# A decode step of two attention and two MLP layers on one core: each layer gets its own list of loads of keys and values, with second copies of some blocks in DRAM

## The chip, the cores and the metric

The kernel runs on one core of one Trainium2 chip. The time is the device time of one execution in microseconds (us). Before the change it is 1343.44 us, the median of 3 runs (1343.42 to 1343.6). In the profile TensorE is PE, its weight loads PEld, VectorE DVE, ScalarE ACT, GpSimd POOL, and the engine that issues most DMAs SP. All rows of the profile come from one profiled execution.

## What is computed

One token of width 640 passes through attention, an MLP, the same attention again and the same MLP again. Both attention layers read the same cache of keys and the same cache of values: 32 heads, 8192 positions, 128 wide, in float32, 134 MB each.

```python
H, Sk, Dh = 32, 8192, 128           # x is (1, 1, 640)
def _A_ref(x, k_cache, v_cache, wq, wo):
    q = heads_of(x @ wq)
    scores = jnp.einsum("bhqd,bhkd->bhqk", q, k_cache) * (Dh ** -0.5)
    p = _softmax(scores, axis=-1)
    o = jnp.einsum("bhqk,bhkd->bhqd", p, v_cache)
    return joined(o) @ wo
def _B_ref(x, w1, w2):
    return jnp.maximum(x @ w1, 0) @ w2

x = x + _A_ref(_layernorm(x), k_cache, v_cache, wq, wo)
x = x + _B_ref(_layernorm(x), w1, w2)
x = x + _A_ref(_layernorm(x), k_cache, v_cache, wq, wo)
x = x + _B_ref(_layernorm(x), w1, w2)
```

## The kernel before

**What is loaded.** The cache doesn't fit into SBUF, so all of it is read from DRAM in the first layer and, but for a part that stays, once more in the second. A head has 8.4 MB: four pieces of keys and four of values, each 128 partitions by 2048 elements (1024 KB). A load ("unit") is one DMA that moves several pieces, with one contiguous row for each partition: 6 pieces are a load of 128x12288 elements (6144 KB), 4 are 128x8192 (4096 KB), 2 are 128x4096 (2048 KB). The host lays the cache out in DRAM in the order of the units, so that each unit is one block there. `UNITS` lists the units of each head, the same for both layers: by pieces or parts of them for heads 0, 1, 28, 29, 30 and 31, whole keys and whole values for heads 2, 3 and 24 to 27, and for heads 4 to 23 units that run over the ends of heads (`PAIR`, `TRIPLE`).

**The order of heads** is `HEADS`: 0 to 31 in the first layer; 31 down to 24, 12 to 23, 4 to 11, 3, 2, 1, 0 in the second. Heads 30 and 31 and three small units of head 29 (`KEPT`) stay in SBUF from the first layer to the second. Most of the first piece of head 24's keys is parked in PSUM by ACT (`PARKED`, lines 526 and 195) and copied back in the second layer, so that its load there is 128x6272 instead of 128x8192.

**The ring.** Units go to a ring of 4248 places of 8 elements a partition. `place` finds room: units of 12288 elements in three slots of 1536 places (the third reaches into the place of `w2`, which is free in the middle of a layer), smaller ones wherever they fit. `pump` issues the next loads on SP's queue, in the order of `todo`, as far as `place` finds room; `release` is called behind the last instruction that reads a piece, frees its place and calls `pump`. So a load is issued when PE has read what lay in its place; nothing else holds it, but for the eight DMA semaphores, which are used in turn.

**The work of a head.** `scores` (line 516) multiplies the pieces of the keys by the query on PE; the maximum, the exponentials and the transposes run on DVE and ACT (lines 531, 545, 552); `values` (line 570) multiplies the pieces of the values; `output` (lines 587 to 614) joins them. Between these stand small steps of the next queries (440, 454), of the output projection (621, 482) and of the MLP's weights (672). The MLP closes each layer. The weights of queries and projections are loaded by ACT's queue into `both_t`, one group of four heads ahead. The MLP's `w2` is loaded into the ring at each layer's end, and while the first layer's MLP runs, four units of head 29 for the second layer are loaded beside the ring (line 231).

Of the kernel before, what the change touches and what calls it, by code (L numbers as in the profile page):

```python
# [15 lines left out]
P = 128  # L16
D = 640
H = 32
SK = 8192
# [21 lines left out]
UNITS = {h: WHOLE for h in range(H)}  # L41
UNITS[0] = HALVES[:2] + LAST
UNITS[1] = HALVES
UNITS[29] = [
# [10 lines left out]
]  # L55
UNITS[30] = HALVES
UNITS[28] = [("k", K_ALL[:1]), ("k", K_ALL[1:2])] + HALVES[1:]
UNITS[31] = HALVES[:2] + LAST
# [5 lines left out]
TRIPLE = [  # L64
    [(0, "k", K_ALL), (0, "v", V_ALL[:2])],
    [(0, "v", V_ALL[2:]), (1, "k", K_ALL)],
    [(1, "v", V_ALL), (2, "k", K_ALL[:2])],
    [(2, "k", K_ALL[2:]), (2, "v", V_ALL)],
]
UNITS = {  # L70
    h: [[(h, kind, piece) for piece in pieces] for kind, pieces in units]
    for h, units in UNITS.items()
}
OWNER = {h: h for h in range(H)}
for first, together in [(4, TRIPLE), (7, TRIPLE), (10, PAIR)] + [(h, TRIPLE) for h in (12, 15, 18, 21)]:
    for h in range(first, first + len(together) - 1):
        UNITS[h], OWNER[h] = [], first
    UNITS[first] = [
        [(first + i, kind, piece) for i, kind, pieces in unit for piece in pieces]
        for unit in together  # L80
    ]
ORDER = [(h, i) for h in range(H) for i in range(len(UNITS[h]))]
HEADS = [list(range(H)), [*range(31, 23, -1), *range(12, 24), *range(4, 12), 3, 2, 1, 0]]
GROUPS = [[heads[a] // HG for a in range(0, H, HG)] for heads in HEADS]
KEPT = [(29, 0), (29, 1), (29, 6)]
BY_WO = KEPT[0]
# [7 lines left out]
PARKED = (24, 0)  # L94
# [8 lines left out]
def size(u):  # L103
    return sum(wide(kind, piece) for _, kind, piece in UNITS[u[0]][u[1]])
# [22 lines left out]
def decode_kernel(ctx: ExitStack, tc: tile.TileContext, x, kv, wq, wo, wqo, w1, w2, out):  # L127
# [15 lines left out]
    kept = [u for u in ORDER if u[0] > KEPT[0][0] or u in KEPT]  # L143
# [16 lines left out]
    def place(layer, u, n):  # L160
# [8 lines left out]
        if layer == 0 and u in kept and (u in KEPT or u[0] == 30 and UNITS[30][u[1]][0][1] == "k"):  # L169
            low, high = (EDGE, RING) if u in KEPT else (FLAT, EDGE)  # L170
# [8 lines left out]
    def pump():  # L179
        while todo:  # L180
# [7 lines left out]
            stays = PARK_ROW if (layer, u) == (1, PARKED) else 0  # L188
# [69 lines left out]
    def pieces_of(L, h, kind):  # L258
# [3 lines left out]
        if L:  # L262
            units.sort(key=lambda i: (h, i) not in kept)
# [876 lines left out]
```

## Time and profile before

| | |
|---|---|
| time, median of 3 runs | 1343.44 us |
| profiled execution, span | 1340.6 us |
| outside the span (the difference) | 2.8 us |
| mean granted clock of TensorE | 0.820 |
| busy: PE, PEld, DVE, ACT | 874.0, 255.5, 290.2, 62.6 us |
| DMA traffic | 571.70 MB in 24546 packets |

The first layer's attention and MLP end at about 704 us of the span, the second's at its end. The span is that of the profiled execution alone, and the times of the runs are measured around it. Of the view by lines, the two groups that fill PE are the keys and the values:

```profile
L516 PE MATMUL ps<-ring,spread_q 128*32 128x512 f32 (+3 forms) x2088 | 332.7, 727 | 149.2 <-DMA ring<-in_kv 148.6
L570 PE MATMUL outs<-ring,p 128*4 128x512 f32 (+3 forms) x2080 | 310.6, 732 | 164.1 <-DMA ring<-in_kv 95.7
```

The columns are line, engine, operation, what is written and read, the count; behind the bar the busy time and the mean in ns; then the idle time of the engine before them, and what ended most of it.

### The profile page before, as it was taken

What the parts mean: (1) busy time and instruction counts of PE and PEld (TensorE: products, weight loads), DVE (VectorE), ACT (ScalarE), POOL (GpSimd) and SP (SyncE); (2) the same over time, 40 slices, a digit from 0 to 9 for tenths busy, and PEclk for the clock granted to TensorE, in tenths of its full rate; (3) what the DMA queues carried; (4) which work ended last, traced back from release to release, by engine and by line L of the source; (5) the groups of instructions that cost most, each with busy time, mean ns of one, the idle gap of its engine ahead of it and who ended that gap; (6) DMA issues with size and microseconds to landing.
All of it is one profiled execution on the core that took longest, in us unless ns stands there. A gap on an engine that the chain in (4) does not pass through costs nothing.

```text
span 1340.6 us, 13403 instructions
## 1 busy us (share of the span) xinstructions
PE 874.0 (65%) x5806; PEld 255.5 (19%) x5806; DVE 290.2 (22%) x956; ACT 62.6 (5%) x155; POOL 2.9 (0%) x10
## 2 busy tenths in 40 slices
PE   5463575767657656676688755657566666567687
PEld 2110121111111111112243211112111111111123
DVE  2120121211212112223123212221221212212222
ACT  0000000000000000000000000000000000000000
POOL 0000000000000000000000000000000000000000
PEclk8686787988777887788799977887778787888789
DMA  9999999999999999999999999999999999999998
GB/s 395 431 435 430 442 423 437 429 428 437 432 434 429 428 439 426 433 425 415 425 396 425 430 435 433 432 433 431 433 429 434 432 428 433 437 427 436 425 424 333
DMA packets 24546, 571.70 MB, mean 426 GB/s; under 512 B 2724, under 2 KB 2984, under 8 KB 6952
## 3 DMA queue, kind: packets, MB, share of 16 engines
q1 hardware_dynamic: 21464, 529.31, 92.1%
q10 hardware_dynamic: 3024, 41.53, 7.3%
q8 instruction: 46, 0.75, 0.2%
q14 instruction: 12, 0.10, 0.0%
HBM read 570.83 MB, written 0.00 MB: 426 GB/s over the span
## 4 chain that ended last, share of the span: by engine, by line
DMA 67%; PE 27%; DVE 4%; ACT 1%; issue 1%; SPq 0%; ACTq 0%; DVEq 0%
DMA ring<-in_kv 66%; PE ps L516 10%; PE outs L570 9%; PE side L672 1%; DMA ring<-in_w 1%; DVE p L591 1%; PE acc L621 1%; PE side L440 1%; ACT p L545 1%; DVE h_t L531 1%; PE small L536 1%; PE small L604 1%; PE side L454 1%; DVE p L552 0%; DVE h_t L537 0%
## 5 line engine op out<-in xcount | busy, mean ns | idle before, releaser
L516 PE MATMUL ps<-ring,spread_q 128*32 128x512 f32 (+3 forms) x2088 | 332.7, 727 | 149.2 <-DMA ring<-in_kv 148.6
L570 PE MATMUL outs<-ring,p 128*4 128x512 f32 (+3 forms) x2080 | 310.6, 732 | 164.1 <-DMA ring<-in_kv 95.7
L531 DVE TENSOR_REDUCE h_t<-ps 128x1 f32<-128x512 f32 x64 | 44.3, 691 | 365.4 <-PE ps L516 365.4
L570 PEld LDWEIGHTS outs<-ring,p 128*4 128x4 f32 x2080 | 50.6, 95 | 348.4 <-issue 233.8
L516 PEld LDWEIGHTS ps<-ring,spread_q 128*32 128x32 f32 x2088 | 63.9, 124 | 277.5 <-issue 188.8
L545 ACT ACTIVATE p<-ps,h_t 128x512 f32<-128x512 f32 x63 | 43.3, 687 | 1161.2 <-DVE h_t L537 1161.2
L552 DVE STREAM_TRANSPOSE p<-p 128x128 f32<-128x128 f32 x256 | 79.8, 312 | 63.9 <-ACT p L545 57.2
L587 DVE TENSOR_SCALAR p<-outs,ind 128x128 f32<-128x128 f32 x64 | 22.5, 351 | 317.2 <-PE outs L570 317.2
L604 PE MATMUL small<-ones,p 128*128 128x1 f32 (+1 forms) x128 | 25.3, 267 | 97.4 <-DVE p L591 97.4
L591 DVE SCALAR_TENSOR_TENSOR p<-outs,ind,p 128x128 f32<-128x128 f32 x188 | 66.0, 351 | 6.7
L536 PE MATMUL small<-ident,h_t 128*128 128x128 f32 x128 | 32.7, 339 | 40.1 <-DVE h_t L531 39.9
L604 PEld LDWEIGHTS small<-ones,p 128*128 128x128 f32 x128 | 19.9, 195 | 159.7 <-DVE p L591 158.9
L672 PE MATMUL side<-w_t,wct 128*128 128x448 f32 (+1 forms) x80 | 45.3, 651 | 0.0
L452 DVE TENSOR_SCALAR q_row<-side,ln_r 128x128 f32<-128x128 f32 x56 | 19.5, 349 | 106.0 <-PE ps L516 59.0
L440 PE MATMUL side<-both_t,ln_xc 128*32 128x512 f32 x140 | 37.3, 844 | 0.0
L536 PEld LDWEIGHTS small<-ident,h_t 128*128 128x128 f32 x128 | 20.0, 196 | 89.0 <-DVE h_t L531 85.5
L621 PE MATMUL acc<-both_t,o_cols 128*64 128x320 f32 x220 | 34.6, 458 | 0.0
L454 PEld LDWEIGHTS side<-sel,q_row 128*128 128x128 f32 x112 | 19.3, 216 | 56.3 <-DVE q_row L452 29.9
L537 DVE TENSOR_REDUCE h_t<-small 128x1 f32<-128x128 f32 x64 | 18.7, 292 | 35.4 <-PE small L536 35.4
L454 PE MATMUL side<-sel,q_row 128*128 128x1 f32 x112 | 24.1, 284 | 0.3 <-DVE q_row L452 0.2
L621 PEld LDWEIGHTS acc<-both_t,o_cols 128*64 128x64 f32 x220 | 15.5, 147 | 29.4 <-issue 17.7
L672 PEld LDWEIGHTS side<-w_t,wct 128*128 128x128 f32 x80 | 13.5, 211 | 32.4 <-issue 32.4
(148 smaller groups left out, 219.5 us busy)
## 6 DMA issues: line engine op xcount, KB each, us to landing
ring<-in_kv SPq DMA_DIRECT2D x50, 6144.0 KB, 35.0
ring<-in_kv SPq DMA_DIRECT2D x23, 4096.0 KB, 33.2
ring<-in_kv SPq DMA_DIRECT2D x29, 2048.0 KB, 27.7
both_t<-in_wqo ACTq DMA_DIRECT2D x12, 2560.0 KB, 24.7
ring<-in_kv SPq DMA_DIRECT2D x4, 5120.0 KB, 34.6
ring<-in_kv SPq DMA_DIRECT2D x9, 1024.0 KB, 23.9
w_t<-in_w ACTq DMA_DIRECT2D x1, 4320.0 KB
ring<-in_kv SPq DMA_DIRECT2D x5, 768.0 KB, 29.5
```

The lines of the kernel that those rows point to most:

```text
L440: nc.tensor.matmul(pq[32 * strip : 32 * strip + 32], xc[:, c : c + 1].to_broadcast([P, 32]), wq_t[:, c], start=c < 4, stop=c in (1, 2, 3, ...
L454: nc.tensor.matmul(mine[:, :1], row, one_of_each, start=True, stop=True, skip_group_check=True)
L516: nc.tensor.matmul(hd.ps[32 * g : 32 * g + 32, c : c + n], spread_q[:, 3 - r : 35 - r], tile_of[:, at + g * n : at + (g + 1) * n], start=f ...
L531: nc.vector.tensor_reduce(hd.nm, hd.ps, AX.X, ALU.max, negate=True)
L536: nc.tensor.matmul(pt[:, :P], hd.nm.to_broadcast([P, P]), ident, start=True, stop=True)
L545: nc.scalar.activation(hd.p, hd.ps, AF.Exp, bias=hd.low, scale=scale, accum_out=hd.l)
L552: nc.vector.transpose(hd.all_p[:, b * P : (b + 1) * P], hd.p[:, b * P : (b + 1) * P])
L570: nc.tensor.matmul((hd.out if r0 < 2 else hd.out_2)[32 * g : 32 * g + 4, r0:r1].rearrange("p r d -> p (r d)"), hd.all_p[:, 32 * i : 32 * i ...
L591: nc.vector.scalar_tensor_tensor(oc, hd.out[:, r], ind[:, r : r + 1], oc, op0=ALU.mult, op1=ALU.add)
L604: nc.tensor.matmul(pt[:, :n], part, mask.to_broadcast([P, n]), start=i == 0, stop=i == len(parts) - 1,)
L621: nc.tensor.matmul(acc[64 * g : 64 * g + 64, : 2 * DR], col.to_broadcast([P, 64]), wt[:, 2 * DR * g : 2 * DR * (g + 1)], start=first, stop ...
L672: nc.tensor.matmul(pt[:, :n], wct[:, c], w1_t[:, c, f : f + n], start=(c == 0), stop=(c == NB - 1),)
```

## The change

The list of units is no longer one for both layers. `FIRST` and `SECOND` are the loads of the two layers, each a list of units, and `UNIT` holds what each unit consists of. A new function `cut` lays the pieces of several heads in a line and cuts it into units of six pieces (6144 KB), also across the ends of heads.

- First layer: heads 0 to 3 are one line, cut into a first unit of two pieces and five of six (before: single loads of 256 to 4096 KB). Heads 24 to 26 are four units of six (before: six units of 4096 KB). Heads 27 to 31 are as before.
- Second layer: heads 29 and 28 are as before. Heads 27, 26 and 25 are four units of six, in the order in which this layer takes them; head 24 is as before. Heads 3 and 2 are units of 6, 6 and 4 pieces, the keys of head 1 are one unit of 4096 KB, and its values and head 0 are as before.
- Heads 10 and 11 are units of 6, 6 and 4 pieces in both layers (before: 5, 5 and 6).

A block that is cut differently in the two layers lies in DRAM twice: this holds for heads 0 to 3 and 24 to 27, 67 MB more in DRAM. The bytes that are loaded are the same, and so is the order of heads. The loads of keys and values on SP are 116 instead of 130: 63 instead of 73 in the first layer, 53 instead of 57 in the second.

```diff
-UNITS = {h: WHOLE for h in range(H)}
-UNITS[0] = HALVES[:2] + LAST
-UNITS[1] = HALVES
+SIX = 6
+UNIT = {}
+def pieces_in_line(heads):
+    return [(h, kind, piece) for h in heads for kind, all_of in (("k", K_ALL), ("v", V_ALL)) for piece in all_of]
+def units_of(h, units):
+    n = sum(u[0] == h for u in UNIT)
+    for i, unit in enumerate(units):
+        UNIT[h, n + i] = unit
+    return [(h, n + i) for i in range(len(units))]
+def alone(h, units):
+    return units_of(h, [[(h, kind, piece) for piece in pieces] for kind, pieces in units])
+def cut(heads, first=0):
+    line = pieces_in_line(heads)
+    ends = [0] * bool(first) + [*range(first, len(line), SIX), len(line)]
+    return units_of(heads[0], [line[a:b] for a, b in zip(ends, ends[1:])])
...
-PAIR = [
-    [(0, "k", K_ALL), (0, "v", V_ALL[:1])],
-    [(0, "v", V_ALL[1:]), (1, "k", K_ALL[:2])],
-    [(1, "k", K_ALL[2:]), (1, "v", V_ALL)],
-]
...
+MIDDLE = [cut(heads) for heads in ([4, 5, 6], [7, 8, 9], [10, 11], [12, 13, 14], [15, 16, 17], [18, 19, 20], [21, 22, 23])]
...
+FIRST = cut([0, 1, 2, 3], 2) + sum(MIDDLE, []) + cut([24, 25, 26]) + alone(27, WHOLE) + sum(ENDS.values(), [])
+KEPT = [(29, 0), (29, 1), (29, 6)]
+SECOND = [u for u in ENDS[29] if u not in KEPT] + ENDS[28] + cut([27, 26, 25])
+PARKED += alone(24, WHOLE)[:1]
+SECOND += [PARKED[1], (24, PARKED[1][1] + 1)]
+SECOND += sum(MIDDLE[3:] + MIDDLE[:3], []) + cut([3, 2])
+SECOND += alone(1, [("k", K_ALL)] + HALVES[2:]) + alone(0, HALVES[:2] + LAST)
+ORDER = list(UNIT)
...
-    todo = [(0, u) for u in ORDER if u != BY_WO]
+    todo = [(0, u) for u in FIRST if u != BY_WO]
     n_first = len(todo)
-    todo += [(1, (h, i)) for h in HEADS[1] for i in range(len(UNITS[h])) if (h, i) not in kept]
+    todo += [(1, u) for u in SECOND]
...
-    kv = np.empty(H * P * SK * 2, k.dtype)
+    kv = np.empty(8 * P * sum(size(u) for u in ORDER), k.dtype)
```

Three places of SP's queue show what moves. At the program's start, before (`in_wq` and `in_wo` are the first query and projection weights, `in_kv` the cache):

```order
L274 DMA both_t<-in_wq 128x2560
L189 DMA ring<-in_kv 128x4096 x3
L189 DMA ring<-in_kv 128x2048
L189 DMA ring<-in_kv 128x1536
L189 DMA ring<-in_kv 128x512
L189 DMA ring<-in_kv 128x4096 x4
L286 DMA both_t<-in_wo 128x2560
L189 DMA ring<-in_kv 128x8192 x4
```

and with the change:

```order
L282 DMA both_t<-in_wq 128x2560
L201 DMA ring<-in_kv 128x4096
L201 DMA ring<-in_kv 128x12288 x2
L294 DMA both_t<-in_wo 128x2560
L201 DMA ring<-in_kv 128x12288 x13
```

Heads 0 to 3 take 14 loads before and 6 with the change, of which the first is the same. The second half of head 0's keys now comes in one load with all of its values.

At the start of the second layer, before (the first rows are the end of head 29 and head 28, then heads 27 to 24, and from 12288 on head 12 and the next):

```order
L189 DMA ring<-in_kv 128x1536
L189 DMA ring<-in_kv 128x2048
L189 DMA ring<-in_kv 128x4096
L189 DMA ring<-in_kv 128x2048 x2
L189 DMA ring<-in_kv 128x4096 x3
L189 DMA ring<-in_kv 128x8192 x6
L189 DMA ring<-in_kv 128x6272
L189 DMA ring<-in_kv 128x8192
L189 DMA ring<-in_kv 128x12288 x24
```

and with the change:

```order
L201 DMA ring<-in_kv 128x1536
L201 DMA ring<-in_kv 128x2048
L201 DMA ring<-in_kv 128x4096
L201 DMA ring<-in_kv 128x2048 x2
L201 DMA ring<-in_kv 128x4096 x3
L201 DMA ring<-in_kv 128x12288 x4
L201 DMA ring<-in_kv 128x6272
L201 DMA ring<-in_kv 128x8192
L201 DMA ring<-in_kv 128x12288 x26
```

Six loads of heads 27 to 25 became four. The first of the six was placed over values of head 30; the first of the four takes that place and the next 512 places, where the last values of head 29 lie.

At the second layer's end, before (heads 10 and 11 from the rows of 10240 on, then 3, 2, 1 and 0):

```order
L189 DMA ring<-in_kv 128x12288 x24
L189 DMA ring<-in_kv 128x10240 x2
L189 DMA ring<-in_kv 128x12288
L189 DMA ring<-in_kv 128x8192 x4
L189 DMA ring<-in_kv 128x4096 x7
L189 DMA ring<-in_kv 128x2048
L189 DMA ring<-in_kv 128x1536
L189 DMA ring<-in_kv 128x512
L222 DMA ring<-in_w 128x1920
```

and with the change:

```order
L201 DMA ring<-in_kv 128x12288 x26
L201 DMA ring<-in_kv 128x8192
L201 DMA ring<-in_kv 128x12288 x2
L201 DMA ring<-in_kv 128x8192 x2
L201 DMA ring<-in_kv 128x4096 x5
L201 DMA ring<-in_kv 128x2048
L201 DMA ring<-in_kv 128x1536
L201 DMA ring<-in_kv 128x512
L234 DMA ring<-in_w 128x1920
```

Of head 1's keys, which came in two halves of 128x4096, one load of 128x8192 is left. On PE four matmuls of head 0's last values are gone, since that piece is no longer cut; DVE, ACT and POOL have the same instructions in the same order.

More of the change, by code (lines that the diff above doesn't have):

```diff
@@ L55 @@
 ]
-UNITS[30] = HALVES
-UNITS[28] = [("k", K_ALL[:1]), ("k", K_ALL[1:2])] + HALVES[1:]
-UNITS[31] = HALVES[:2] + LAST
-PAIR = [
-    [(0, "k", K_ALL), (0, "v", V_ALL[:1])],
-    [(0, "v", V_ALL[1:]), (1, "k", K_ALL[:2])],
-    [(1, "k", K_ALL[2:]), (1, "v", V_ALL)],
-]
[L64 to L72, printed above, removed]
-}
[L74 to L82, printed above, removed]
+MIDDLE = [cut(heads) for heads in ([4, 5, 6], [7, 8, 9], [10, 11], [12, 13, 14], [15, 16, 17], [18, 19, 20], [21, 22, 23])]
+ENDS = {
+    28: alone(28, [("k", K_ALL[:1]), ("k", K_ALL[1:2])] + HALVES[1:]),
+    29: alone(29, SPLIT),
+    30: alone(30, HALVES),
+    31: alone(31, HALVES[:2] + LAST),
+}
+PARKED = [(24, 0)]
+FIRST = cut([0, 1, 2, 3], 2) + sum(MIDDLE, []) + cut([24, 25, 26]) + alone(27, WHOLE) + sum(ENDS.values(), [])
[6 more added lines that the diff above has]
+ORDER = list(UNIT)
 HEADS = [list(range(H)), [*range(31, 23, -1), *range(12, 24), *range(4, 12), 3, 2, 1, 0]]
 GROUPS = [[heads[a] // HG for a in range(0, H, HG)] for heads in HEADS]
-KEPT = [(29, 0), (29, 1), (29, 6)]
 BY_WO = KEPT[0]
@@ L103, in size @@
 def size(u):
-    return sum(wide(kind, piece) for _, kind, piece in UNITS[u[0]][u[1]])
+    return sum(wide(kind, piece) for _, kind, piece in UNIT[u])
 F_ROWS = [448, 448, 416, 416]
@@ L168, in place @@
             step, high = BIG, 3 * BIG
-        if layer == 0 and u in kept and (u in KEPT or u[0] == 30 and UNITS[30][u[1]][0][1] == "k"):
+        if layer == 0 and u in kept and (u in KEPT or u[0] == 30 and UNIT[u][0][1] == "k"):
             low, high = (EDGE, RING) if u in KEPT else (FLAT, EDGE)
@@ L187, in pump @@
             o = dram_at[u]
-            stays = PARK_ROW if (layer, u) == (1, PARKED) else 0
+            stays = PARK_ROW if (layer, u) == (1, PARKED[1]) else 0
             nc.sync.dma_start(
@@ L238, in load_beside @@
         load_into(u, where, nc.sync)
[L239 removed]
+        for t, (_, kind, piece) in enumerate(UNIT[u]):
             at_of[layer, u, t] = where, at
@@ L258, in pieces_of @@
     def pieces_of(L, h, kind):
-        owner = OWNER[h]
-        units = list(range(len(UNITS[owner])))
-        if L:
-            units.sort(key=lambda i: (h, i) not in kept)
-        for i in units:
-            for t, (of, its, piece) in enumerate(UNITS[owner][i]):
+        for u in kept + SECOND if L else FIRST:
+            for t, (of, its, piece) in enumerate(UNIT[u]):
                 if (of, its) == (h, kind):
-                    yield piece, (L, (owner, i), t)
+                    yield piece, (L, u, t)
     both_t = wts.tile([P, 2 * HG * D], F32, name="both_t")
@@ L523, in scores @@
             )
-        if where == (0, PARKED, 0):
+        if where == (0, PARKED[0], 0):
             for a, bank in parked:
@@ L1076, in _laid_out @@
         a = 0
-        for h, kind, piece in UNITS[u[0]][u[1]]:
+        for h, kind, piece in UNIT[u]:
             if kind == "k":
```

8 lines of the change are left out of this document (3 added, 5 removed).

## The prediction

> **What bounds the kernel now.** I read the page first: the span, the line of DMA shares, the queues, and the chain that ended last.
>
> ```profile
> span 1340.6 us, 13403 instructions
> DMA  9999999999999999999999999999999999999998
> q1 hardware_dynamic: 21464, 529.31, 92.1%
> q10 hardware_dynamic: 3024, 41.53, 7.3%
> DMA 67%; PE 27%; DVE 4%; ACT 1%; issue 1%; SPq 0%; ACTq 0%; DVEq 0%
> ```
>
> The second line is the mean busy share of the core's 16 DMA engines in 40 slices: nine tenths or more in all but the last. The queues say it sharper. The packets of SP's queue (q1) and of ACT's (q10) took 92.1% and 7.3% of what 16 engines have in the span, 99.4% together, so about 0.6% (8 us) is left, and part of that is the start and the end, where no load can run. The chain is loads of the cache for two thirds. The kernel is a stream of loads that never stops. What can move its end is the bytes (unchanged), the cost of a load besides its bytes, and a moment at which the queue runs dry.
>
> How far is it from running dry? The page's issue table gives the median time from issue to landing:
>
> ```profile
> ring<-in_kv SPq DMA_DIRECT2D x50, 6144.0 KB, 35.0
> both_t<-in_wqo ACTq DMA_DIRECT2D x12, 2560.0 KB, 24.7
> ```
>
> Next, what a load takes by itself. In the timeline of PE these rows began when a load landed (start, duration, ..., in brackets the idle time and its releaser). The first three belong to consecutive loads of 6144 KB with no other load between, the last two to loads of 4096 KB:
>
> ```profile
> 969.36 1.06 PE L516 MATMUL ps<-ring,spread_q 128*32 128x512 f32 x8 [1.54 <-DMA ring<-in_kv]
> 983.90 3.60 PE L570 MATMUL outs<-ring,p 128*4 128x512 f32 x16 [1.20 <-DMA ring<-in_kv]
> 998.43 5.27 PE L570 MATMUL outs<-ring,p 128*4 128x512 f32 x32 [4.05 <-DMA ring<-in_kv]
> ...
> 598.40 5.34 PE L516 MATMUL ps<-ring,spread_q 128*32 128x512 f32 x32 [2.06 <-DMA ring<-in_kv]
> 608.14 5.31 PE L570 MATMUL outs<-ring,p 128*4 128x512 f32 x32 [3.09 <-DMA ring<-in_kv]
> ```
>
> A load of 6144 KB takes 14.53 us ((998.43 - 969.36) / 2), one of 4096 KB 9.74. So a 6144 KB load is issued, in the median, 35.0 - 14.5 = 20.5 us before the engines get to it. For 2048 KB the timeline of SP serves: at the first layer's end eight loads are under way, and SP's next issue waits for the landing of the one eight before:
>
> ```profile
> 664.69 5.22 SPq L222 DMA_DIRECT2D ring<-in_w  x2
> 674.48 0.33 SPq L222 DMA_DIRECT2D wct<-in_w  x1
> ```
>
> Two landings of 2048 KB lie between 664.69 and 674.48: 4.895 us each.
>
> **The change, part by part.**
>
> *Fewer loads.* The trace counts 130 loads on this line:
>
> ```profile
> L189 SPq DMA_DIRECT2D ring<-in_kv x130: 327/328/1540, 1.2 to 1296.9; - x130
> ```
>
> The change leaves 116, so 14 fewer with the same bytes. Three loads of 2048 KB take 3 x 4.895 = 14.685 us, the one of 6144 KB with the same bytes 14.53: two loads fewer save 0.155, or 0.08 a load. From the larger sizes, 3 x 9.74 - 2 x 14.53 = 0.16 for one load fewer; this difference hangs on one spacing rounded to 0.01, so I take 0.08 and keep 0.16 as the upper end. 14 x 0.08 = **1.1 us gained** (0 if all of it were hidden, 2.2 at 0.16), 0.8 of it in the first layer (10 loads) and 0.3 in the second (4). [...]
>
> *Program's start.* The first load is the same; the second half of head 0's keys now waits for a load of 6144 KB. PE will stand still until that lands, some 10 us later than before. It costs nothing if the queue stays full:
>
> ```profile
> 13.26 3.64 PE L516 MATMUL ps<-ring,spread_q 128*32 128x512 f32 x16 [0.47 <-DVE spread_q L504]
> ```
>
> PE has read the first half of the keys at 16.9 us, and that releases the fourth cache load. By then 1.3 MB of query weights, 2.1 + 6.3 + 6.3 MB of cache and twice 1.3 MB of weights are issued, 18.6 MB, which at 6.29 MB in 14.53 us keep the engines busy until about 43: 26 us of cover. The fifth waits for head 0's values, about 41 by an estimate (landing near 27, then a head's keys, softmax and values), with the queue full until about 59. Without that cover each us would cost one. I take 0.
>
> *Heads 24 to 26 in the first layer, and 10, 11, 3 and 2.* Units of six in three slots, as in the middle of a layer, where the 20.5 us above are the cover. A coarser slot comes free up to one half-unit (7 us) later, which leaves 13. At the first layer's end the loads are the same as before, and their pace is set by landings, as the two SP rows show. ACT's weight loads take turns with longer rows of the cache now, but their 24.7 us are those beside units of six already. I take 0 for all of these, and +0.5 as their upper end.
>
> *The second layer's start* is the one place without cover. These rows are the SP timeline and the loads that it issued at 726.5, then PE's last values of head 29, then what the engines do when a load comes late:
>
> ```profile
> 719.62 21.58 SPq L189 DMA_DIRECT2D ring<-in_kv  x3
> ...
> L189 SPq DMA_DIRECT2D ring<-in_kv x1: 328/328/328, 726.5 to 726.5; - x1
> DMA to landing us min/median/max: 25.6/25.6/25.6
> ...
> 737.19 3.62 PE L570 MATMUL outs<-ring,p 128*4 128x128 f32 x40 [0.74 <-DVE p L552]
> ...
> 692.60:693.60 1.00, 1.00 (x14) 0.74 (x6) 0.69 (x4) 0.37 (x2) 0.00 (x0) 1.00 0.53 208
> ```
>
> Three issues: head 28's last load at 719.62, head 27's keys at 726.5, its values at 740.87 (719.62 + 21.58 less one issue of 0.33), right behind head 29's values on PE, which end at 740.81. With the change there is no load at 726.5; the first unit of six needs the place of those values, so it is issued at 740.87. When is the queue empty then? Head 27's keys landed at 726.5 + 25.6 = 752.1 and took 9.74, so head 28's last load landed at 742.4. The new load is thus issued 1.5 us ahead of the end of the queue. The last row is a window at a moment when the queue did run dry (an issue at 692.67): for 1 us the share of the engines falls to 0.53 until the new packets flow, so issue to packets takes about 1 us, and 1.5 us of lead just suffices where all engines end together. They don't: some end up to a us early. I take **0.3 us lost**, with 0 and 0.8 as ends (0.8 is a late issue like that one, with half of each of two us lost). Both sides of this race come 0.8 us earlier with the first term, so it stays. Behind it the lead is back: the next issue (746.5 before, when head 28's keys are read) meets a queue full until 742.7 + 14.5 = 757.
>
> *The second layer's end.* Head 1's keys come whole. Before, PE took their first half early:
>
> ```profile
> L189 SPq DMA_DIRECT2D ring<-in_kv x1: 328/328/328, 1269.0 to 1269.0; - x1
> DMA to landing us min/median/max: 27.9/27.9/27.9
> ...
> 1295.16 1.80 PE L516 MATMUL ps<-ring,spread_q 128*32 128x512 f32 x8
> 1297.78 3.25 PE L516 MATMUL ps<-ring,spread_q 128*32 128x512 f32 x24
> 1311.68 1.06 PE L516 MATMUL ps<-ring,spread_q 128*32 128x512 f32 x8
> 1316.48 1.93 PE L516 MATMUL ps<-ring,spread_q 128*32 128x512 f32 x16 [0.26 <-DMA ring<-in_kv]
> 1321.50 0.61 PE L570 MATMUL outs<-ring,p 128*4 128x256 f32 x8 [0.91 <-DMA ring<-in_kv]
> 1335.70 1.27 PE L482 MATMUL side<-ring,hT 128*32 128x160 f32 x24 [0.19 <-DMA ring<-in_w]
> 1336.90 0.47 PE L935 MATMUL side<-ring,hT 64*32 64x160 f32 x8
> ```
>
> The second half landed at 1269.0 + 27.9 = 1296.9, which is where the whole lands now (less the terms above). PE starts at 1296.9 instead of 1295.16, 1.8 us late, and has no slack up to head 0's keys at 1311.68, which it enters without a wait. Behind that its waits for loads are 0.26, 0.91 and 0.19, and the 24 matmuls at 1335.70 hold about 0.25 more (three times 0.34, the pace of the row's neighbours at full clock, is 1.02 of the 1.27): 1.6 us in all. So 1.8 - 1.6 = 0.2 us reaches the last matmul. I take **0.2 lost**; 0 at the low end, and 1.6 if head 1's keys run at the pace of their first row throughout (1.80 per 8 instead of 3.25 per 24, some 2 us more, of which a part meets waits).
>
> *Sum*: -1.1 + 0.3 + 0.2 = -0.6 us. The profiled span goes from 1340.6 to 1340.0; with the 2.8 us around it, the time from 1343.44 to **1342.8 us**. A measurement of this kernel can tell about 0.2% (2.7 us) from no change, so this counts as no difference.
>
> **The rivals.**
>
> *The first unit of six comes late, and the kernel is slower.* The lead at 741 is PE's work on heads 31 to 29:
>
> ```profile
> 705.00:741.00 36.00, 31.00 (x322) 11.76 (x318) 12.25 (x42) 2.42 (x6) 0.55 (x1) 1.00 1.02 429
> 741.00:760.00 19.00, 14.37 (x100) 4.55 (x102) 5.63 (x19) 0.78 (x2) 0.00 (x0) 0.91 0.99 424
> ```
>
> PE is busy 31.0 of 36 us there at a granted clock of 1.00 (the figure behind the brackets). At the 0.91 of the next window these would be 34.1, head 29's values would end 3.1 us later, and from 0.5 us on every us is a us without loads, where the old kernel had 9.7 us more to move. -1.1 + 0.3 + 3.1 + 0.2 = +2.5: 1345.9 us. It turns into a loss when PE is more than about 0.6 us later than in this execution. Against it: nothing in the change slows PE ahead of 741, and the clock was full throughout. 10%.
>
> *The end is bound by PE.* Clock or chores make head 1 later than my 0.2: -1.1 + 0.3 + 1.6 = +0.8, 1344.2 us. For it: PE enters head 0 without slack. Against it: the clock was 1.00 or close to it right there. 10%.
>
> *A load's fixed cost is paid in full.* The shortest loads of the page that met a nearly empty queue:
>
> ```profile
> ring<-in_w SPq DMA_DIRECT2D x4, 320.0 KB, 4.4
> ```
>
> Their bytes take about 0.8 us, so 3.6 is not bytes; 14 x 3.6 = 50 us, 1293. [...] Against it: 2 MB loads landed every 4.895 us with no such pause. 1%.
>
> *Larger loads gain more than their count*, at 0.16 a load and with both losses at 0: 1343.44 - 2.2 = 1341.2. 10%. *The change does nothing*, every removed load's cost having been hidden: 1343.4 + 0.5 = 1343.9. 7%.
>
> **How the numbers follow.** My forecast has 62%, the rivals 10, 10, 1, 10 and 7. The range goes from the gain at its upper end, 1341.2, to the first rival, 1345.9. Faster by more than 0.2% means below 1340.7: the third rival and a part of the fourth, should 0.16 be too small, 5%. Slower means above 1346.1: half of the first rival and a cover that I have misjudged, 8%. The rest, 87%, is no difference.
>
> **What would show it.** In the profile after: 116 loads on the line; the spacing of landings unchanged at 14.53; no slice of the DMA line below nine tenths but the last; PE idle near 17 to 27 us without cost. At 741 a window of 1 us with the DMA share between 0.6 and 1, and the first unit of six landing near 757 less 0.8; a share of 0 for several us there is the first rival. At the end, head 1's keys starting with a wait for a load, and PE's later waits shrinking. The prediction is wrong if the 6144 KB spacing changes, or if the queue runs dry in the stretch of heads 24 to 26 or at the start.

## The result, and the profile after

The change makes the kernel slower by about a quarter of a per cent: 1346.61 us, the median of 7 runs (1346.15 to 1348.17), beside 1343.42 for the kernel before (7 runs). The ratio is 1.0024, with a 95% interval from 1.0014 to 1.0033. Forecast were 1342.8 and a range that ended at 1345.9. The profiled execution took 1346.2 us with a span of 1344.4, 3.8 more than before. Of all executions below, one of e17 (2566 us) and one of the kernel before beside it (1612 us) stand far apart from the others and are left out.

The page of the changed kernel: span, DMA share in 40 slices, the two queues (packets, MB, share of 16 engines), the chain, and the median time from issue to landing of the large loads.

```profile
span 1344.4 us, 13358 instructions
...
DMA  9999999999999999999999999999999999999997
...
q1 hardware_dynamic: 19448, 529.31, 91.8%
q10 hardware_dynamic: 3024, 41.53, 7.3%
...
DMA 65%; PE 29%; DVE 4%; ACT 1%; issue 1%; ACTq 0%; DVEq 0%; SPq 0%
...
ring<-in_kv SPq DMA_DIRECT2D x67, 6144.0 KB, 34.5
```

By its form this is the kernel before: same bytes, same bound. Only q1's share is 0.3% lower: 1344.4 x 0.3% = 4 us more in which no load ran. The 40 slices are too coarse to show where. The loads of the cache, and the rows of PE that began when loads of 6144 KB landed:

```profile
L201 SPq DMA_DIRECT2D ring<-in_kv x116: 327/328/1492, 1.2 to 1299.2; - x116
```

```profile
971.84 1.94 PE L524 MATMUL ps<-ring,spread_q 128*32 128x512 f32 x8 [3.21 <-DMA ring<-in_kv]
...
1000.90 5.67 PE L578 MATMUL outs<-ring,p 128*4 128x512 f32 x32 [4.46 <-DMA ring<-in_kv]
```

116 loads, and (1000.90 - 971.84) / 2 = 14.53 us each: both as forecast. So the loss is not in the loads but between them. These are windows of 1 us at the second layer's start, first of before, then of after (length; busy PE, PEld, DVE, ACT, POOL; granted clock; DMA share; GB/s):

```profile
739.00:740.00 1.00, 1.00 (x16) 0.23 (x11) 0.00 (x0) 0.00 (x0) 0.00 (x0) 1.00 1.19 508
740.00:741.00 1.00, 0.81 (x8) 0.00 (x0) 0.12 (x1) 0.00 (x0) 0.00 (x0) 1.00 1.15 492
741.00:742.00 1.00, 0.00 (x0) 0.00 (x0) 0.93 (x3) 0.00 (x0) 0.00 (x0) 1.00 1.02 426
```

```profile
739.00:740.00 1.00, 1.00 (x16) 0.21 (x8) 0.00 (x0) 0.00 (x0) 0.00 (x0) 1.00 0.43 180
740.00:741.00 1.00, 0.47 (x8) 0.00 (x0) 0.43 (x2) 0.00 (x0) 0.00 (x0) 1.00 0.19 82
741.00:742.00 1.00, 0.00 (x0) 0.00 (x0) 0.93 (x3) 0.00 (x0) 0.00 (x0) 1.00 1.61 492
```

The engines run dry from 739 us on, at a granted clock of 1.00. (Share and GB/s count a packet with all its time and bytes where it begins, so a share can pass 1: the last row has ten packets of 49152 bytes, which begin at 741.48 and later and end from 743.8 on.) In a window of 30 us around it, before and after, the single packets matter less:

```profile
725.00:755.00 30.00, 23.24 (x228) 8.51 (x224) 10.52 (x34) 1.56 (x4) 0.00 (x0) 1.00 1.02 433
```

```profile
725.00:755.00 30.00, 22.82 (x220) 8.30 (x212) 10.64 (x34) 1.55 (x4) 0.00 (x0) 1.00 0.96 399
```

30 x (1 - 399/433) = 2.4 us. A second count, without windows, agrees. It spreads each packet's bytes evenly over its time, and compares the moments at which the two kernels have moved the same number of bytes: between 735 and 760 us the changed kernel falls 2.5 us behind. Why so early? SP's issues of head 28's last load (719.3) and of the first unit of six (740.5), each with its time to landing, and PE's last values of head 29, in the changed kernel:

```profile
L201 SPq DMA_DIRECT2D ring<-in_kv x1: 328/328/328, 719.3 to 719.3; - x1
...
DMA to landing us min/median/max: 22.5/22.5/22.5
...
L201 SPq DMA_DIRECT2D ring<-in_kv x1: 328/328/328, 740.5 to 740.5; - x1
```

```profile
736.85 3.62 PE L578 MATMUL outs<-ring,p 128*4 128x128 f32 x40 [0.74 <-DVE p L560]
```

PE and SP are where the prediction had them: the values end at 740.47, the unit is issued at 740.5, and head 28's last load lands at 719.3 + 22.5 = 741.8. That is a lead of 1.3 us, as forecast. But that landing is the moment at which the last of 16 engines was done. Worked out from the records of the single engines, the first was done with that load at 739.44, the mean one at 740.40, the last at 741.75; the new unit's packets began between 741.48 and 742.46, 0.95 to 1.9 us behind the issue. Measured by the mean engine there was no lead at all. By the packets' records the engines stood still for 1.9 us each on the mean. The rest of the loss is that the first sixteen packets of the new unit took 1.9 to 3.2 us each, where 8482 of the 8576 packets of this size in the trace took 1.8.

There is a second, smaller loss. Head 12's first load is issued at 822.8 instead of 814.9, because its place is now freed by a later unit, and in the window from 815 to 835 the rate is 414 GB/s, where it was 442:

```profile
815.00:835.00 20.00, 14.34 (x96) 3.46 (x99) 5.61 (x19) 1.56 (x4) 0.00 (x0) 0.77 0.99 414
```

20 x (1 - 414/442) = 1.3 us (1.2 by the second count, between 815 and 840 us). Last, the second layer's end, rows of PE after (head 1's keys, then head 0's keys and values, then the last product):

```profile
1299.26 1.93 PE L524 MATMUL ps<-ring,spread_q 128*32 128x512 f32 x8 [3.64 <-DMA ring<-in_kv]
...
1302.00 2.79 PE L524 MATMUL ps<-ring,spread_q 128*32 128x512 f32 x24
...
1320.27 1.93 PE L524 MATMUL ps<-ring,spread_q 128*32 128x512 f32 x16 [0.25 <-DMA ring<-in_kv]
...
1325.27 0.61 PE L578 MATMUL outs<-ring,p 128*4 128x256 f32 x8 [0.90 <-DMA ring<-in_kv]
```

PE waits for head 1's keys, and its later waits are what they were (0.25 and 0.90, before 0.26 and 0.91). So PE adds nothing in this execution; the loads come later, and PE with them. The span's account: 0.6 gained in the first layer (head 28's last load landed at 742.4, now 741.8), 2.4 and 1.3 lost in the two holes, and 0.8 because the slowest engine ends further behind the mean one at the end (3.35 us instead of 2.52, from the engines' records): +3.9, where the spans differ by 3.8. The last part is scatter rather than the change: over the profiles of all runs that distance goes from 2.2 to 3.4 us.

### The profile page after: what moved, and what is told of

Same layout as the page of the kernel before. It is cut to its first block, busy times and chain, and to the rows that moved or that the text cites. A ratio compares the mean times of both kernels' runs of the same rounds, so it can differ in the third digit from the quotient of the medians.

```text
span 1344.4 us, 13358 instructions
## 1 busy us (share of the span) xinstructions
PE 882.2 (66%) x5798; PEld 256.6 (19%) x5798; DVE 290.1 (22%) x956; ACT 62.6 (5%) x155; POOL 2.9 (0%) x10
## 4 chain that ended last, share of the span: by engine, by line
DMA 65%; PE 29%; DVE 4%; ACT 1%; issue 1%; ACTq 0%; DVEq 0%; SPq 0%
DMA ring<-in_kv 63%; PE ps L524 10%; PE outs L578 10%; PE acc L629 2%; PE side L680 2%; PE side L448 1%; DVE p L599 1%; DMA ring<-in_w 1%; ACT p L553 1%; DVE h_t L539 1%; PE small L544 1%; PE side L462 1%; PE small L612 1%; DVE p L560 1%; DVE p L595 0%
## 5 line engine op out<-in xcount | busy, mean ns | idle before, releaser
L578 PE MATMUL outs<-ring,p 128*4 128x512 f32 (+2 forms) x2072 | 315.8, 744 | 182.5 <-DMA ring<-in_kv 104.1
L448 PE MATMUL side<-both_t,ln_xc 128*32 128x512 f32 x140 | 30.9, 693 | 0.0
L629 PEld LDWEIGHTS acc<-both_t,o_cols 128*64 128x64 f32 x220 | 15.9, 151 | 29.1 <-issue 17.1
```

The source lines that it names most:

```text
L448: nc.tensor.matmul(pq[32 * strip : 32 * strip + 32], xc[:, c : c + 1].to_broadcast([P, 32]), wq_t[:, c], start=c < 4, stop=c in (1, 2, 3, ...
L578: nc.tensor.matmul((hd.out if r0 < 2 else hd.out_2)[32 * g : 32 * g + 4, r0:r1].rearrange("p r d -> p (r d)"), hd.all_p[:, 32 * i : 32 * i ...
L629: nc.tensor.matmul(acc[64 * g : 64 * g + 64, : 2 * DR], col.to_broadcast([P, 64]), wt[:, 2 * DR * g : 2 * DR * (g + 1)], start=first, stop ...
```

## The experiments

Theory A: the price is the queue that runs dry behind head 29's values. Theory B: it is the place of the second copies in DRAM. The runs added a theory C, another part of the change, because with the hole gone a second thing remained. "Late" counts executions of 1345 us or more.

| run | loads | median us | lowest to highest, n | late | ratio, 95% interval |
|---|---|---|---|---|---|
| e1_start_undone | 118 | 1344.65 | 1342.56 to 1348.65, 11 | 5 | 1.0011, 1.0002 to 1.002 |
| e2_start_alone | 128 | 1347.8 | 1347.25 to 1349.0, 5 | 5 | 1.0034, 1.0022 to 1.0046 |
| e3_small_first | 117 | 1344.85 | 1343.19 to 1348.69, 12 | 6 | 1.0014, 1.0005 to 1.0023 |
| e4_copies_alone | 130 | 1343.63 | 1342.97 to 1344.59, 11 | 0 | 1.0001, 0.9992 to 1.0009 |
| e5_both_undone | 120 | 1346.68 | 1342.24 to 1350.92, 12 | 7 | 1.0019, 1.0007 to 1.0031 |
| e6_halves_back | 118 | 1343.94 | 1342.41 to 1348.87, 12 | 5 | 1.0009, 0.9998 to 1.002 |
| e7_end_alone | 128 | 1344.2 | 1343.04 to 1348.91, 11 | 3 | 1.0004, 0.9995 to 1.0013 |
| e8_key_whole | 118 | 1344.47 | 1342.68 to 1348.92, 11 | 4 | 1.0012, 1.0003 to 1.0021 |
| e9_first_end_undone | 120 | 1344.33 | 1342.28 to 1350.06, 12 | 5 | 1.0011, 1.0001 to 1.002 |
| e10_first_end_alone | 128 | 1343.06 | 1342.67 to 1344.67, 11 | 0 | 0.9999, 0.9991 to 1.0008 |
| e11_cut_start_left | 118 | 1348.0 | 1345.55 to 1353.22, 6 | 6 | 1.0048, 1.0032 to 1.0063 |
| e12_change_again | 116 | 1347.1 | 1345.43 to 1354.07, 6 | 6 | 1.0036, 1.0021 to 1.0051 |
| e13_low_alone | 122 | 1343.38 | 1342.68 to 1349.06, 12 | 3 | 1.0006, 0.9997 to 1.0015 |
| e14_pair_alone | 130 | 1343.35 | 1342.61 to 1344.95, 11 | 0 | 0.9998, 0.999 to 1.0007 |
| e15_low_undone | 126 | 1343.15 | 1342.35 to 1345.1, 11 | 1 | 0.9997, 0.9988 to 1.0005 |
| e16_head0_undone | 122 | 1343.1 | 1342.22 to 1346.34, 11 | 2 | 1.0, 0.9991 to 1.0008 |
| e17_hole_left | 124 | 1347.35 | 1345.05 to 1351.49, 5 | 5 | 1.0032, 1.002 to 1.0045 |
| e18_low_undone_again | 126 | 1343.02 | 1342.35 to 1346.43, 11 | 1 | 0.9999, 0.999 to 1.0007 |

Beside them the kernel before ran at 1343.36 to 1343.54 in the median, 9 of 146 executions late.

**The hole: undo it, make it alone, fill it.**

```diff
 # e1_start_undone: heads 27, 26, 25 whole again
-SECOND = [...] + ENDS[28] + cut([27, 26, 25])
+SECOND = [...] + ENDS[28] + sum([alone(h, WHOLE) for h in (27, 26, 25)], [])
 # e2_start_alone: the kernel before, and only this
+SECOND += cut([27, 26, 25]) + HIGH[24]
 # e3_small_first: a first unit of two pieces, then six
+SECOND = [...] + ENDS[28] + cut([27, 26, 25], 2)
 # e4_copies_alone: the kernel before, heads 0 to 3 and 24 to 27 of the second layer from copies in the same cuts
```

> The change, but heads 27, 26 and 25 in the second layer come as whole keys and whole values again (six loads of 4096 KB from second copies); 118 loads. Theory A (the queue runs dry at 739 to 742 us, because the first unit of six waits for the last values of head 29, and again at 823 to 826): both holes gone, time 1342.5 to 1343.3, a little below the kernel before. Rival B (the second copies or their place in DRAM are slower to read): still 1346.0 to 1347.0, since all copies stay. Rival C (the end: head 1's keys in one load make PE late): still 1346.0 to 1347.0.

> The kernel before, but heads 27, 26 and 25 in the second layer come as four units of six from second copies; all else as before; 128 loads. Theory A: the same two holes, time 1345.5 to 1347. Rival B: copies of three heads of eight, about 1344.5, with longer packets and no hole. Rival C: 1343.4, as before.

> The change, but the line of heads 27, 26 and 25 in the second layer begins with a unit of two pieces (2048 KB), then 6, 6, 6 and 4; 117 loads. The small unit fits over values of head 30, so it is issued near 726 us and gives the queue 4.9 us more before the first unit of six is needed; and the last unit holds only values, so that head 12's first unit waits for less work of PE. Theory A: no hole, 1342.4 to 1343.2. Rivals B and C: 1346.0 to 1347.0.

> The kernel before with its own cuts, but heads 0 to 3 and 24 to 27 are read in the second layer from second copies in DRAM (67 MB more in DRAM); 130 loads. Theory A: no difference, 1343.0 to 1343.9. Rival B: 1345.5 to 1347. Rival C: no difference.

The copies alone cost nothing that can be measured: theory B falls. The cut alone costs 1347.8 - 1343.5 = 4.3 us, more than the whole change. The window around 740 in e2, then with the hole undone in e1 and filled by a small load in e3:

```profile
725.00:755.00 30.00, 24.86 (x234) 8.61 (x226) 9.09 (x29) 1.56 (x4) 0.00 (x0) 0.96 0.93 384
```

```profile
725.00:755.00 30.00, 23.24 (x226) 8.19 (x218) 10.49 (x33) 1.55 (x4) 0.00 (x0) 1.00 1.02 435
```

```profile
725.00:755.00 30.00, 23.23 (x227) 8.23 (x216) 10.49 (x33) 1.56 (x4) 0.00 (x0) 1.00 1.03 439
```

In e2 30 x (1 - 384/433) = 3.4 us are lost, in e1 and e3 nothing. Theory A stands for the hole at 740; the second one is not in e2 (441 GB/s from 815 to 835 us), and its 1347.8 us lie above what theory A gave it. The fastest execution of each kernel with the hole (the change, e2, e11, e12, e17) is at 1345.1 to 1347.3 us, of each without it at 1342.2 to 1343.2. But the medians of e1 and e3 miss theory A's ranges by more than 1 us: they bring back only 2 of the 3.2 us, and about half of their executions are late by 2 to 5 us, the rest about as fast as before. Something else is in the change that strikes in some executions only.

**What strikes.** The second layer's end was the first suspect.

```diff
 # e5_both_undone: the whole second layer cut as before
 # e6_halves_back: e3, and head 1's keys in halves
-SECOND += alone(1, [("k", K_ALL)] + HALVES[2:]) + alone(0, HALVES[:2] + LAST)
+SECOND += alone(1, HALVES) + alone(0, HALVES[:2] + LAST)
 # e7_end_alone: the kernel before, and only cut([3, 2]) and head 1's keys whole
 # e8_key_whole: e3, and heads 3 and 2 whole
-SECOND += sum(MIDDLE[3:] + MIDDLE[:3], []) + cut([3, 2])
+SECOND += sum(MIDDLE[3:] + MIDDLE[:3], []) + alone(3, WHOLE) + alone(2, WHOLE)
```

> The changed kernel with the whole of its second layer's list as before: heads 27, 26 and 25 as loads of 8192, heads 3 and 2 as loads of 8192, head 1's keys in two loads of 4096 (120 loads). Left of the change are the first layer's list and the copies in DRAM. The kernel with heads 27, 26, 25 undone alone ran from 1342.6 to 1348.7 where the kernel before ran from 1343.0 to 1346.1. Theory A2 (the rest comes from the second layer's end: by heads 3, 2 and 1's larger loads TensorE starts its last heads later and the end then hangs on TensorE, whose clock differs from run to run): the scatter is gone, 1343.0 +- 0.3, span about 1340.3 and the end again about 3.8 us after the last landing. Theory C (the rest comes from the first layer, its larger loads at heads 24 to 26 or its small first load): it stays, runs between 1342.5 and 1348.5 with a median of about 1344.6.

> The changed kernel with head 27's keys cut so that the units of six start with one of two blocks (as the run with a small first load), and with head 1's keys in two loads of 4096 again (118 loads); heads 3 and 2 stay cut in six, six and four. Theory A2 with head 1's whole keys as what makes TensorE late: no scatter, 1343.0 +- 0.4. Theory A2 with heads 3 and 2 as what makes it late, or theory C: like the run with a small first load, 1343.2 to 1348.7, median 1344.8.

> The kernel before with only the second layer's end of the change: heads 3 and 2 in loads of six, six and four blocks and head 1's keys as one load of 8192, from copies of their own in DRAM (128 loads); the first layer and the second layer's start as before. Theory A2: the scatter shows here too, from 1343 to 1348 with a median of 1344 to 1345, and in the profile TensorE no longer waits for loads behind head 1's keys. Theory C: 1343.3 +- 0.4 and no scatter.

> The changed kernel with a small first load of the units of six for heads 27, 26, 25, and with heads 3 and 2 as loads of 8192 again; head 1's keys stay one load of 8192 (118 loads). Theory A2 with head 1's whole keys as the cause: 1343.2 to 1348.7, median about 1344.8. Theory A2 with heads 3 and 2 as the cause: 1343.0 +- 0.4 and no scatter. Theory C: like the run with a small first load, median 1344.8.

None made the late executions go, e5 least of all, which has nothing of the change left but the first layer's list, heads 10 and 11, and the copies. So the second layer's end is not what makes them late (e7, by itself, has 3 of 11 late and a median inside theory A2's range, but its profile loses its time elsewhere, as follows). The end has a price of its own in some executions: in e1's profile (1344.21 us) PE takes its last rows without a wait for a load, and the span ends 5.4 us behind the landing of the last weights, where it was 3.8 before; in e3's 4.4. In these four runs the profile fell on late executions, e5's at 1348.57 us. Windows at the end of the first layer, first of before, then of e5:

```profile
691.30:698.20 6.90, 6.16 (x123) 4.63 (x126) 2.23 (x12) 0.37 (x2) 0.00 (x0) 1.00 0.90 329
698.20:715.30 17.10, 15.75 (x176) 7.41 (x180) 4.78 (x22) 0.87 (x2) 1.10 (x2) 1.00 1.01 410
```

```profile
691.30:698.20 6.90, 5.32 (x102) 4.09 (x102) 2.01 (x11) 0.37 (x2) 0.00 (x0) 1.00 0.87 301
698.20:715.30 17.10, 16.92 (x114) 8.49 (x118) 1.80 (x11) 0.00 (x0) 1.10 (x2) 0.50 0.78 281
```

The granted clock is 0.50 for 17.1 us between the layers. There PE's work is what frees the places for the second layer's loads: e5's timeline of SP has the first of them at 711.20, where it was 705.24 before.

```profile
711.20 10.71 SPq L201 DMA_DIRECT2D ring<-in_kv  x4
```

281 GB/s instead of 410 tell the price: 17.1 x (1 - 281/410) = 5.4 us. All four profiles of e5 to e8, late without the hole, have the half clock there, for 13.7 to 17.1 us, and by the second count lose 3.4 to 5.9 us between 700 and 720; none of the other sixteen has it, and none of those loses more than 0.4 us there. What goes ahead of it? PE's rows on the MLP's last small load, in before, e1, e5 and e8 in this order:

```profile
697.43 0.75 PE L482 MATMUL side<-mix,hT 128*32 128x160 f32 x16 [0.42 <-DMA mix<-in_w]
```

```profile
697.87 0.75 PE L490 MATMUL side<-mix,hT 128*32 128x160 f32 x16 [0.98 <-DMA mix<-in_w]
```

```profile
698.38 1.29 PE L490 MATMUL side<-mix,hT 128*32 128x160 f32 x16 [1.76 <-DMA mix<-in_w]
```

```profile
697.61 0.75 PE L490 MATMUL side<-mix,hT 128*32 128x160 f32 x16 [0.85 <-DMA mix<-in_w]
```

PE idles for this load 1.76 us in e5, 1.61 in e6, 1.82 in e7 and 0.85 in e8, and the half clock starts at 698.2 to 699.3. In the other profiles the wait is 0.33 to 0.56, but for e1 with 0.98, where the clock stayed full. In e5 fifteen engines had ended this load by 697.16 and one at 698.34 (from the engines' records), in e7 fifteen by 697.64 and one at 699.05; in e6 two were late, in e8 none stands out.

By the clock records of before and of the changed kernel the granted clock stands at 1.00 and at 0.50 in turn, in 162 and 150 stretches, and each but the last, at the span's end, lasts 1 to 26 steps of 3.41 us. Over all 20 profiles it fell from full to half 1638 times, and by the profiles' busy times of PE this can be sorted. Behind a step in which PE was busy for less than 1.4 us it fell in 979 of 981 cases, and behind one with 2.4 us or more in 2 of 1731. Between the layers that step had 1.81 us of work in e5, 1.99 in e6, 1.96 in e7 and 2.56 in e8; in e1 it had 2.43, and the clock stayed full. So the wait for the late load brings the step's work near the stretch between the two counts (1.4 to 2.4 us), but doesn't decide alone; what does is open.

The 17.1 us are five of these steps. e15 and e18, the same kernel, have their steps 1.1 us apart against the span's start; that this would let one execution meet the half clock and the next not is an estimate from this one distance. In e5 the clock fell behind a step in which PE had been busy for 1.81 us, about half of it, and it stayed at half while PE was busy for 16.92 of 17.10 us.

**Which part makes it more frequent.**

```diff
 # e9_first_end_undone: e6, and the first layer's heads 24 to 26 whole; e11: the change, and this
-FIRST = cut([0, 1, 2, 3], 2) + sum(MIDDLE, []) + cut([24, 25, 26]) + alone(27, WHOLE) + [...]
+FIRST = cut([0, 1, 2, 3], 2) + sum(MIDDLE, []) + sum([alone(h, WHOLE) for h in (24, 25, 26, 27)], []) + [...]
 # e10_first_end_alone: the kernel before, and only cut([24, 25, 26]) in the first layer
 # e12_change_again: the changed kernel
```

> The changed kernel with the first layer's heads 24 to 26 as loads of 8192 again, a small first load for the second layer's heads 27, 26 and 25, and head 1's keys in halves (120 loads); the run with head 1's keys in halves differs from it by heads 24 to 26 of the first layer alone. The slow executions met so far have the granted clock at 0.50 from about 698 to 714 us, between the layers, where the queue then runs dry for 3 to 4 us; 45% of the executions with the new first layer end 2.3 us or more late, and 7% of those with the old one. Theory T1 (units of six at heads 24 to 26 bring TensorE's work closer to the first layer's end, and the denser work meets the throttle there more often): executions of 1345.5 or more become rare again, at most 2 of some 12, median 1342.8 +- 0.4. Theory T2 (another part of the first layer's list, heads 0 to 3 or heads 10 and 11, or chance): 4 to 6 of 12 stay above 1345.5, median 1344 +- 1.

> The kernel before with only the first layer's heads 24 to 26 in units of six (128 loads); the second layer reads copies of heads 24 to 27 in loads of 8192 as before, which alone ran as the kernel before does. Theory T1: 4 to 6 of some 12 executions end at 1345.5 or later, with the granted clock at 0.50 at about 700 us where the profile is of one of those; the rest run at 1343.2 +- 0.4. Theory T2: at most 1 or 2 of 12, median 1343.4 +- 0.3.

> The changed kernel with the first layer's heads 24 to 26 as loads of 8192 again (118 loads); the second layer's heads 27, 26 and 25 stay in units of six from the first on. Theory A with T1 (the hole at 740 and the one at 824 are one cause, worth 2.5 to 3.5, the throttle between the layers is another): tight executions around 1346.0 +- 0.5, both holes in the profile. If the holes come about only when TensorE is late from the first layer: 1343.0 and no hole.

> The changed kernel itself, to see how its executions spread on the same chip as the three others. Theory A with T1: about half at 1346.2 to 1346.8 (the holes without the throttle), the other half 1 to 4 us later where the clock is halved between the layers too; median about 1347. If the throttle between the layers does not add to the holes: all within 1346 to 1348.2, as the seven runs so far.

Heads 24 to 26 are not it: undone, 5 of 12 stay late; alone, none is. Theory T1 falls. e11 and e12 spread from 1345.4 to 1354 us, wider than the first seven runs of the change. The profile of e12 (1347.99 us) shows a further place where time can go: at the first layer's end, from 632 to 644 us, it falls 2.8 us behind the kernel before. PE comes 3.4 us later to the values there (632.25 instead of 628.89), and with it the next load (638.96 instead of 635.81). So not every late execution need be one with the half clock between the layers.

```diff
 # e13_low_alone: the kernel before, and only cut([0, 1, 2, 3], 2) in the first layer
 # e14_pair_alone: the kernel before, and only heads 10 and 11 as six, six, four
 # e15_low_undone (and e18): e6, and the first layer's heads 0 to 3 as before; e17: the change, and this
-FIRST = cut([0, 1, 2, 3], 2) + [...]
+FIRST = alone(0, HALVES[:2] + LAST) + alone(1, HALVES) + alone(2, WHOLE) + alone(3, WHOLE) + [...]
 # e16_head0_undone: e6, and head 0 as before
+FIRST = alone(0, HALVES[:2] + LAST) + cut([1, 2, 3]) + [...]
```

> The kernel before with only the first layer's heads 0 to 3 in units of six behind a first load of two blocks (122 loads); the second layer reads the old blocks. In the profiles of kernels with this list the clock is first halved at 35 to 44 us where the old list has 20 to 25, and the order of halved stretches that follows is another. Theory P1 (heads 0 to 3 of the first layer: by the other start the halved stretches fall otherwise, and more often on the stretch between the layers): 4 to 6 of some 12 executions at 1345 or later, with the clock at 0.50 at 700 us if the profile is of one of them, the others at 1343.1 +- 0.4 (8 loads of 0.04 fewer). Theory P2 (heads 10 and 11) or P3 (copies and second layer): at most 1 of 12 at 1345 or later, median 1343.1 +- 0.3.

> The kernel before with only heads 10 and 11 in loads of six, six and four blocks in both layers, where it was five, five and six (130 loads, no second copies). Theory P1: at most 1 of 12 at 1345 or later, median 1343.4 +- 0.3. Theory P2: 4 to 6 of 12 at 1345 or later.

> The changed kernel with the first layer's heads 0 to 3 as before, a small first load for the second layer's heads 27, 26 and 25, and head 1's keys in halves (126 loads). Theory P1: executions of 1345 or more are rare (at most 2 of 12), median 1343.0 +- 0.4: that is then the best of the versions without the hole at 740. Theory P2 or P3: 4 to 6 of 12 at 1345 or later, median about 1344.

> As the run with the first layer's heads 0 to 3 undone (1343.15, 1 of 11 executions at 1345 or later), but heads 1 to 3 are in units of six again; head 0 keeps its six loads as before (122 loads). Theory P1a (it is the program's start, the loads of head 0 and with them TensorE's first work, that sets how the halved stretches fall): at most 2 of 12 at 1345 or later, median 1343.0 +- 0.4, and the first halved stretch at 20 to 25 us. Theory P1b (the units of six of heads 1 to 3): 4 to 6 of 12 at 1345 or later, first halved stretch at 35 us or more in a part of them.

> The changed kernel with only the first layer's heads 0 to 3 as before (124 loads): the second layer's heads 27, 26, 25 are in units of six from the first on, as in the change. With both theories (hole at 740 and 824 always; halved clock between the layers mostly by heads 0 to 3): tight, 1345.4 to 1347.8 with a median of about 1346.3, both holes in the profile, none above 1349. Were the hole only a consequence of the throttle: 1343.2.

> The run with the first layer's heads 0 to 3 undone, a small first load and head 1's keys in halves (126 loads), once more for its interval: 1343.1 +- 0.3, 0.3 below the kernel before, at most 2 of 12 at 1345 or later. If its tight executions were chance, 4 to 6 of 12 are late and the median is about 1344.

With the change's head 0 and no hole (e1, e3, e5, e6, e8, e9, e13) 35 of 82 executions are late; with head 0 as before and no hole (e4, e7, e10, e14 to e16, e18) 7 of 77; in the kernel before 9 of 146. With head 1's keys in halves on both sides it is 20 of 47 (e5, e6, e9, e13) against 4 of 66. So it is the loads of heads 0 to 3 in the first layer. That it is head 0's, and that the units of six of heads 1 to 3 do no harm, rests on e16 with 2 of 11, too few to show it. e13, with this part alone, is the weak point: 3 of 12, between the two expectations. How the program's start reaches a stretch 690 us later is not settled. That the first halved stretch comes later with the new list, as the expectation of e13 had it, holds in some profiles only (35 to 44 us in seven of them, but 20 to 21 in e3, e11 and e13).

e17 was to be tight, below 1349, and wasn't (1345.05 to 1351.49). Its hole is 3.6 us (381 GB/s against 433):

```profile
725.00:755.00 30.00, 24.87 (x226) 8.51 (x218) 9.08 (x29) 1.56 (x4) 0.00 (x0) 0.94 0.92 381
```

```profile
737.69 5.32 PE L578 MATMUL outs<-ring,p 128*4 128x128 f32 x40 [0.74 <-DVE p L560]
```

Head 29's values took 5.32 us instead of 3.62, at half clock, and the unit that waits for them was issued at 743.1. Over the profiles with the hole (after, e2, e11, e12, e17) the loss by this window goes from 1.8 to 3.6 us, and it is above 3 in the two in which the clock was halved for 3.4 us between 720 and 742. By the second count it is 2.3 to 4.1 us, and the lead orders it. Here the lead is how long before the mean engine's end of the load before it a load was issued (negative: behind that end):

| profile | lead of the first unit of six, us | lost from 735 to 760 us | lead of head 12's first load, us | lost from 815 to 840 us |
|---|---|---|---|---|
| after | -0.1 | 2.5 | 1.7 | 1.2 |
| e2 | -1.7 | 4.1 | 5.6 | 0.0 |
| e11 | 0.1 | 2.3 | 4.1 | 0.0 |
| e12 | 0.0 | 2.5 | 3.0 | 0.1 |
| e17 | -1.8 | 4.0 | 2.7 | 0.2 |

At the first unit of six, lead and loss add up to 2.3 to 2.5 us in all five. The second loss is of the same kind: it is there where the lead was 1.7 us, and all but gone from 2.7 on.

With the old cuts, where head 27's keys are already queued, the same half clock costs nothing: e4 has it in this window, and the rate is full:

```profile
740.00:741.00 1.00, 1.00 (x8) 0.15 (x4) 0.00 (x0) 0.00 (x0) 0.00 (x0) 0.50 1.07 459
```

The version without either cause (e15, e18: hole filled, heads 0 to 3 as before) runs at 1343.15 and 1343.02, 0.3 and 0.4 below the kernel before, with intervals that include no change. No version here is faster by more than can be measured.

## Why the prediction was wrong

**The step that failed is the second layer's start**: "1.5 us of lead just suffices where all engines end together. They don't: some end up to a us early. I take 0.3 us lost, with 0 and 0.8 as ends". The lead was about right (1.3 us), and its two other numbers were not; "up to a us" was an estimate that stood on no row. The engines ended up to 2.3 us before the landing, and the packets came 0.95 to 1.9 us after the issue, not 1: the window at 692.67 showed the first packet (693.62, 0.95 us behind its issue), not the last engine's. The term was 2.4 us in the profiled execution and up to 4.1 in others. The mechanism, the queue running dry behind head 29's values, stood among the rivals, but only as a late PE: "Against it: ... the clock was full throughout". It took no late PE, and that the rival's 1345.9 us lies near the 1346.2 of the profiled execution is luck. The prediction's own rows would have shown that there was no lead at the mean engine: the issue was due at 740.87, and 742.4 less some 1.4 us, the distance of the mean engine, is 741.0. The full 2.4 us don't follow from that, since the slow first packets were in no row of the prediction. With 2.4 in place of 0.3 its sum is -1.1 + 2.4 + 0.2 = +1.5, or 1344.9 us, still in the stated range. What took the profiled execution beyond it is the second loss (1.3 us) and the slow last engine (0.8).

**"Behind it the lead is back"** held for the next issue, of which it was said (746.1 us, a full queue), but not for all that follow: head 12's first load came 8 us later and cost 1.3 us in the profiled execution. In the four other profiles with the hole, where that load had more lead, the rate in that window is 432 to 443 GB/s, so this is no fixed cost.

**Fewer loads**: 0.8 us were forecast for the first layer, 0.6 measured by landings (0.4 to 0.5 by the mean engine). By the second count 0.4 to 0.5 us are gained by 60 us already, where heads 0 to 3 have saved their 8 loads: about 0.06 a load, beside 0.08 forecast. The gain does not show in the medians: 8 fewer loads (e16) and 4 (e15, e18) both give 0.3 to 0.4. The term was of the right size or too large, and too small to matter.

**The program's start** was called free because the queue stays full. PE did stand still as forecast:

```profile
28.43 3.64 PE L524 MATMUL ps<-ring,spread_q 128*32 128x512 f32 x16 [11.35 <-DMA ring<-in_kv]
```

and no load was lost there. That the loads of heads 0 to 3 raise the share of late executions to 43%, from 6% in the kernel before and 9% in the runs with the old list was in no term and no rival. **Heads 24 to 26, 10, 11**: taken at 0, and e10 and e14 confirm it. **The end**: +0.2 was forecast; in the changed kernel's profile PE waits for loads there, so the term did not come up. In e1's the end hung on PE, by 1.6 us more than before, as the rival "The end is bound by PE" had it.

Of the 3.2 us, e1 and e3 return about 2 by the hole alone. Most of the rest goes with the late executions: with heads 0 to 3 of the first layer and head 1's halves as before too (e15, e18) the kernel is back at 1343.0 to 1343.2. e15 differs from e6 by the first layer's heads 0 to 3 alone, 0.8 us in the median and 1 late execution of 11 for 5 of 12.

## What to carry to other kernels

Where a stream of loads is the bound, measure the lead of the next load from the mean engine's end, not from the landing, and add the time from issue to packets: here 1.4 and up to 1.9 us, so that 1.5 us of "lead" was a hole of 2.4. In these profiles a lead of some 2.4 to 3 us ahead of the mean engine's end was what it took to lose nothing. The first load behind a tight spot should be small, since its place comes free early (e3 against the change: issued at 725.1 instead of 740.5 us, 439 GB/s instead of 399). Look at the spread of the executions, not at the median alone: a cause that strikes in four of ten executions hides in a median, and whether the profile shows it is luck.

## What the runs showed of the hardware

The figures are worked out from the traces of this case, of the runs named.

- In e5 one engine of 16 ended the MLP's last small load 1.2 us after the fifteen others (698.34 and 697.16), and TensorE stood idle for 1.76 us ahead of its first matmul on it, at 698.38. In the changed kernel the 16 engines' ends of one load of 4096 KB lay 2.3 us apart (739.44 to 741.75).
- In the changed kernel the load that met engines which had run dry paid for more than the gap. The gap was 1.9 us on the mean; the load's first sixteen packets, from 741.48 us on, took 1.9 to 3.2 us each, where 8482 of the 8576 packets of this size in the trace took 1.8; 2.4 us were lost.
- The granted clock was full or half, in stretches of 1 to 26 steps of 3.41 us (before and the changed kernel, 162 and 150 stretches, but for the last of each). Over the 20 profiles it fell to half behind 979 of 981 steps at full clock with PE busy for less than 1.4 us, and behind 2 of 1731 with 2.4 us or more. Each of its 1638 returns to full came behind a step with PE busy for 2.57 us or more, but a busy step was not always enough: in e5 the clock stayed at half for 17.1 us with PE busy for 99% of them.
- A half clock of 3.4 us cost nothing in e4, where head 27's keys were already queued (442 GB/s from 736 to 745 us, the mean of its windows, beside 441 before). In e17, where one load waited for the matmuls that it slowed, 4.0 us were lost, beside 2.5 in the changed kernel at full clock: 1.5 us more.
